# A new order for a PE-bound kernel: PSUM banks from a table, and dummy matmuls one by one

## The chip, the cores and the metric

The kernel runs on one core of one Trainium2 chip. Its time is the device time of one execution in microseconds (us). Three timed runs of the kernel before gave 412.07, 411.61 and 411.92 us, median 411.92. Matmuls run on TensorE (PE), elementwise work on VectorE (DVE), ScalarE (ACT) and GpSimd (POOL); transfers are issued by SyncE (SP) and a few by ACT.

## The reference

Two layers. The first is attention over a sliding window of 64 positions, 8 batches, 8 heads of 64 dimensions, 576 positions. Its output, heads side by side, is x (8 x 576 x 512), the input of a mixture of four experts, each a causal attention with one head; the gate takes the best two of four experts at each position.

```python
scores = scale * q @ k.T;  mask = (rel >= 0) & (rel < 64)
attn = exp(scores - max) / (sum + 1e-9);  x = attn @ v            # layer 1
logits = x @ w_gate;  topk = best 2 of 4;  w = softmax over these # layer 2
for e in range(4):
    a = softmax(causal(scale * (x @ wq[e]) @ (x @ wk[e]).T))
    out += w[e] * (a @ (x @ wv[e]) @ wo[e])       # where e is chosen
```

Everything is float32.

## The kernel before, in words

**Layer 1** (stage 1) works on units of eight tiles. A tile is a pair of heads and a block of 64 query rows; its keys are the block itself and the one before. There are 36 units, u = 0 to 35. `s1_qk(u)` multiplies queries and keys into two PSUM banks. ACT copies the scores of the block before to SBUF (`sm`), DVE adds those of the block itself by a predicated copy (`own` is the mask), DVE takes the row's maximum (`st`), POOL adds it, ACT takes the exponential, DVE sums, ACT and DVE make the reciprocal, POOL multiplies. `s1_t(u)` transposes the result on PE through the identity matrix `ident` (tile `t`); ACT copies it (`ft`), and for the early units DVE and POOL mask it into `pt`. `s1_av(u)` multiplies with the values (tile `o`), and ACT and DVE write the result as a high and a low part in float32r, `xh` and `xl`.

**Layer 2** (stage 2) takes the batches one by one. Each projection is a sum of three float32r products, high by high, high by low, low by high: `v2ps` (values and gate), `kps` and `qps` (keys and queries, two pairs of experts, two halves of the positions). The weights are split once in the same way; `wklo` and `wvlo` are such low parts, written by DVE. Scores (`s` from `kt`, `qt`) go through a custom DVE instruction with the causal mask, ACT's exponential and POOL's multiplication; DVE transposes 32x32 blocks and DMAs move them (`pt` from `st`); a second value product on PE (`o`), and the output projection `ops`. The last batch is transposed on PE.

**What sets the order.** `Plan` records all instructions; matmuls inside one `nc.block` form one entry. `issue()` (line 194 of the profile's file) hands them out in the order of `LIST`, a table with one number for each entry. Every engine executes its own in that order and waits for semaphores; there is no scheduler behind it. In the profile all instructions carry line L203, where `Plan` calls them, so rows are told apart by their tiles.

**PSUM.** Eight banks. All tiles come from one pool with the tag `s` and `bufs=8`; a new tile takes a bank that the pool gives it.

**Dummies.** `warm(k)` issues two matmuls of the identity with itself into a bank that nobody reads; each float32 matmul is two instructions on PE, so one call shows as four. `WARM = 6` calls are in the list, all early.

A name such as `s_3_0` in the order below is `s1_3_0`, the first bank of unit 3's scores (the order drops a digit that follows a letter); the last number counts tiles.

Of the kernel before, what the change touches and what calls it, by code (L numbers as in the profile page):

```python
# [7 lines left out]
F32 = mybir.dt.float32  # L8
# [8 lines left out]
BLK = S // 64  # L17
# [148 lines left out]
)  # L166
TAIL = 2
WARM = 6
BPOS = 0.05
SJOIN = 1  # L170
PARTS = ((0, 5), (5, 9))
# [47 lines left out]
def window_attention_moe_attention(ctx: ExitStack, tc: tile.TileContext, qT, kT, vW,  # L219
# [130 lines left out]
    def tiles(u):  # L350
        for i in range(SIZES[u]):
            yield i % 2, i // 2, *ORDER[STARTS[u] + i]

    def s1_qk(u):

        banks = [psum.tile([128, 4, 128], F32, tag="s", bufs=8, name=f"s1_{u}_{x}") for x in range(2)]
# [612 lines left out]
```

## Time and profile before

| | before |
|---|---|
| median of three timed runs | 411.92 us |
| the profiled execution, whole | 413.24 us |
| its span, first to last instruction | 411.5 us |
| mean granted clock of PE | 0.995 |
| PE busy | 398.9 us, 97% |
| DVE / ACT / POOL busy | 310.7 / 260.5 / 276.7 us |
| dummy matmuls | 24 instructions, 5.2 us |
| DMA | 72.69 MB, 177 GB/s |

The profile shows one execution. PE's matmuls overlap and their ends are modelled, so "busy" says that PE had work and not that it ran at its peak; the time from one start to the next tells the speed. Of the critical chain 87% of the span is PE and 8% DVE. A group "idle before" names what an engine waited for.

### The profile page before, as it was taken

To read this page: it belongs to the slowest core of one execution; us is meant where nothing else is said; L and a number is where in the kernel's file an instruction comes from. 1 tells how busy PE (TensorE), PEld (TensorE's weight loads), DVE (VectorE), ACT (ScalarE), POOL (GpSimd) and SP (SyncE) were. 2 spreads that over 40 slices of the span, in tenths; PEclk is the share of its full clock that TensorE was granted. 3 is DMA by queue.
4 is the path that set the end of the run, shared out by engine and by line. 5 is a ranking of instruction groups with operands and counts; after the bars stand their busy time and mean duration, and the time that the engine had idled before them with its cause. 6 is when DMAs were issued, how large, how long until landed. Compare 5 with 4: busy or idle time off the path is not lost.

```text
span 411.5 us, 14007 instructions
## 1 busy us (share of the span) xinstructions
PE 398.9 (97%) x5308; PEld 358.9 (87%) x5308; DVE 310.7 (75%) x996; ACT 260.5 (63%) x865; POOL 276.7 (67%) x471
## 2 busy tenths in 40 slices
PE   7689999999999999999999999999999999999996
PEld 7479889999988989898989898988988999898875
DVE  3799998889695878879786876969887768445742
ACT  2666657685748485674858567486856676447852
POOL 3868887977797876887786966877768671504420
PEclk9899999999999999999999999999999999999999
DMA  7987346376867475368776669487657613453113
GB/s 240 349 310 268 111 144 231 78 208 181 239 223 203 135 182 217 106 172 267 193 248 143 205 147 308 130 211 197 176 130 222 151 60 80 131 134 103 53 53 127
DMA packets 33363, 72.69 MB, mean 177 GB/s; under 512 B 6160, under 2 KB 10256, under 8 KB 33296
## 3 DMA queue, kind: packets, MB, share of 16 engines
q1 hardware_dynamic: 32640, 71.14, 58.2%
q8 instruction: 42, 0.69, 0.7%
q10 hardware_dynamic: 656, 0.66, 0.5%
q14 instruction: 25, 0.20, 0.2%
HBM read 39.85 MB, written 9.44 MB: 120 GB/s over the span
## 4 chain that ended last, share of the span: by engine, by line
PE 87%; DVE 8%; POOL 2%; ACT 1%; issue 1%; ACTq 0%; POOLq 0%
PE o L203 18%; PE s L203 17%; PE ops L203 12%; PE v2ps L203 12%; PE kps L203 12%; PE qps L203 11%; PE t L203 4%; DVE pt L203 2%; DVE st L203 2%; DVE sm L203 1%; POOL sm L203 1%; PE warm L203 1%; DVE xl L203 1%; ACT sm L203 0%; DVE wklo L203 0%
## 5 line engine op out<-in xcount | busy, mean ns | idle before, releaser
L203 POOL TENSOR_SCALAR p<-p,r,g 128x448 f32<-128x448 f32 (+4 forms) x135 | 84.0, 636 | 29.5 <-DVE r L203 23.8
L203 POOL TENSOR_TENSOR sm<-sm,st 128x512 f32<-128x512 f32 x72 | 76.9, 1070 | 30.1 <-DVE st L203 20.0
L203 POOL TENSOR_SCALAR_AFFINE_SELECT pt<-ft 64x512 f32<-64x512 f32 x126 | 84.2, 668 | 17.5 <-ACT ft L203 8.4
L203 ACT ACTIVATE p<-p,r 128x192 f32<-128x192 f32 (+3 forms) x135 | 78.7, 588 | 16.9 <-DVE r L203 16.7
L203 PE MATMUL o<-pt,v 128*64 128x64 f32 (+2 forms) x1776 | 80.8, 249 | 1.8 <-DVE pt L203 1.2
L203 PEld LDWEIGHTS o<-pt,v 128*64 128x64 f32 x1776 | 68.2, 138 | 15.0 <-issue 3.2
L203 DVE STREAM_TRANSPOSE st<-p 128x128 f32<-128x128 f32 (+5 forms) x126 | 59.9, 515 | 5.7 <-POOL p L203 5.5
L203 DVE CUSTOM_DVE_ANT_0 p<-s,causal 128x320 f32<-128x320 f32 (+2 forms) x120 | 54.3, 483 | 7.8 <-PE s L203 7.3
L203 DVE TENSOR_REDUCE st<-sm 128x8 f32<-128x512 f32 x72 | 48.4, 679 | 7.0 <-ACT sm L203 6.1
L203 PE MATMUL s<-kt,qt 64*128 64x320 f32 (+3 forms) x480 | 43.3, 318 | 0.0
L203 DVE COPY_PREDICATED sm<-own,s 128x256 f32<-128x256 uint8 x72 | 29.3, 442 | 12.9 <-ACT sm L203 7.7
L203 PE MATMUL kps<-xh,wklo 128*128 128x256 f32 (+1 forms) x128 | 37.7, 295 | 1.2 <-DVE wklo L203 1.2
L203 PE MATMUL kps<-xh,wkhi 128*128 128x256 f32 (+1 forms) x128 | 38.7, 302 | 0.0
L203 PE MATMUL qps<-xh,wqhi 128*128 128x320 f32 (+1 forms) x128 | 38.4, 300 | 0.0
L203 PE MATMUL v2ps<-wvhi,xh 128*128 128x260 f32 x128 | 37.7, 294 | 0.2 <-DVE xl L203 0.2
L203 PE MATMUL s<-k,q 64*64 64x128 f32 (+1 forms) x1116 | 37.8, 275 | 0.1
L203 PE MATMUL qps<-xl,wqhi 128*128 128x320 f32 (+1 forms) x128 | 37.6, 294 | 0.0
L203 PE MATMUL kps<-xl,wkhi 128*128 128x256 f32 (+1 forms) x128 | 37.6, 294 | 0.0
L203 PE MATMUL qps<-xh,wqlo 128*128 128x320 f32 (+1 forms) x128 | 37.6, 294 | 0.0
L203 PEld LDWEIGHTS s<-kt,qt 64*128 64x128 f32 x480 | 35.0, 186 | 2.8 <-issue 0.7
L203 PE MATMUL v2ps<-wvhi,xl 128*128 128x260 f32 x128 | 36.2, 283 | 0.0
L203 PE MATMUL v2ps<-wvlo,xh 128*128 128x260 f32 x128 | 36.2, 283 | 0.0
(124 smaller groups left out, 921.6 us busy)
## 6 DMA issues: line engine op xcount, KB each, us to landing
v<-in_vW_dram SPq DMA_DIRECT2D x28, 576.0 KB, 5.2
pt<-st SPq DMA_DIRECT2D x112, 116.0 KB, 2.3
pt<-st SPq DMA_DIRECT2D x112, 80.0 KB, 2.1
out_dram<-out SPq DMA_DIRECT2D x32, 256.0 KB, 2.5
k<-in_kT_dram SPq DMA_DIRECT2D x28, 288.0 KB, 5.0
q<-in_qT_dram SPq DMA_DIRECT2D x28, 288.0 KB, 5.2
v<-in_vW_dram SPq DMA_DIRECT2D x3, 320.0 KB, 5.9
out_dram<-out SPq DMA_DIRECT2D x7, 128.0 KB, 2.5
```

The costliest lines, as they stand in the source:

```text
L203: call(*args, **kw)
```

## The change

- `BANKS`, a string of digits, names the bank of each PSUM tile, in the order in which tiles are made. Each bank has a tag of its own with one buffer (`bank()`), so a tile waits until the tile before it in that bank has been read.
- The scores and the value products of units 0 to 3 are now one list entry for each pair of heads instead of one for all eight tiles (`parts(u)`), so that other work can stand between the pieces.
- `warm(k)` is one matmul instead of two, and `WARM` is 24 instead of 6: 24 dummies in place of 12.
- `LIST` is new from its first number to its last, 2797 entries. So every engine's order differs, in most places by a few positions.

```diff
 LIST = (
-    1, 3, 2, 0, 7, 5, 6, 4, 16, 20, 18, 14, 15, 17, 9, 21, 19, 69, 29, 279, 46, 67, 48, 34, 35, 41, 44, 39, 42, 45,
+    1, 3, 2, 0, 6, 4, 7, 5, 15, 19, 14, 17, 16, 18, 8, 22, 21, 20, 29, 30, 31, 308, 309, 34, 315, 35, 45, 46, 61, 53,
...
+BANKS = (
+    "2150600134050431751546247014523236576301365721057242035652177252136347041470465160577323414673270015"
...
-WARM = 6
+WARM = 24
...
-    psum = ctx.enter_context(tc.tile_pool(name="psum", bufs=2, space=PSUM))
+    psum = ctx.enter_context(tc.tile_pool(name="psum", bufs=1, space=PSUM))
+    numbers = iter(BANKS)
+
+    def bank(shape, name):
+        return psum.tile(shape, F32, tag="s" + next(numbers, "0"), name=name)
...
+    def parts(u):
+        t = list(tiles(u))
+        return [[x for x in t if x[2] == p] for p in sorted({x[2] for x in t})] if u < 4 else [t]
+
     def s1_qk(u):
 
-        banks = [psum.tile([128, 4, 128], F32, tag="s", bufs=8, name=f"s1_{u}_{x}") for x in range(2)]
-        with nc.block("s"):
-            for x, j, p, b in tiles(u):
-                c0 = 64 * int(b == 0)
...
+        banks = [bank([128, 4, 128], f"s1_{u}_{x}") for x in range(2)]
+        for group in parts(u):
+            with nc.block("s"):
+                for x, j, p, b in group:
...
     def s1_av(u):
...
-        with nc.block("a"):
-            for i, (x, j, p, b) in enumerate(tiles(u)):
...
+        for group in parts(u):
+            with nc.block("a"):
+                for x, j, p, b in group:
+                    i = 2 * j + x
...
     def warm(k):
-        ps = psum.tile([128, 512], F32, tag="s", bufs=8, name=f"warm_{k}")
+        ps = bank([128, 512], f"warm_{k}")
         with nc.block("z"):
-            for i in range(2):
-                nc.tensor.matmul(ps[:, 0:128], lhsT=ident, rhs=ident, start=True, stop=True)
+            nc.tensor.matmul(ps[:, 0:128], lhsT=ident, rhs=ident, start=True, stop=True)
```

In all other places `psum.tile(..., tag="s", bufs=8, ...)` becomes `bank(...)`.

**Place 1.** POOL, from the first instruction of the program on; `ident` is the identity that the dummies read, `tri`, `m_f`, `causal` and `below` are constants of the masks. First before:

```order
L203 MEMSET sm_1_115 128x64
L203 ISA
L203 AFFINE_SELECT m_f<-m_f 64x64
L203 MEMSET sm_0_108 128x64
L203 MEMSET sm_1_115 128x64
L203 MEMSET sm_0_108 128x64
L203 MEMSET ident 128x128
L203 AFFINE_SELECT ident<-ident 128x128
L203 MEMSET causal 128x576
```

Now, the same stretch of POOL (`v_1` is a tile for the values of layer 2):

```order
L213 ISA
L213 AFFINE_SELECT tri<-tri 64x64
L213 AFFINE_SELECT m_f<-m_f 64x64
L213 MEMSET causal 128x576
L213 MEMSET ident 128x128
L213 MEMSET v_1_72 64x256
L213 AFFINE_SELECT ident<-ident 128x128
L213 MEMSET sm_1_133 128x64
```

The identity moved behind a select on `tri` and the large fill of `causal`, and a fill of `v_1` stands between its own two instructions; the small fills of `sm` moved behind it.

**Place 2.** PE, around the first transpose `t_0` of stage 1; `s_3` are unit 3's scores, `o_0` is unit 0's value product. First before:

```order
L203 MATMUL warm_101<-ident 128x128 x2
L203 MATMUL t_0_112<-ident,sm_0_108 128x128 x4
L203 MATMUL s_3_0_133<-k_76,q_75 64x128 x2
L203 MATMUL s_3_1_134<-k_76,q_75 64x128 x2
L203 MATMUL s_3_0_133<-k_78,q_77 64x128 x2
...
L203 MATMUL s_3_1_134<-st_69 64x128 x2
L203 MATMUL t_1_122<-ident,sm_1_115 128x128 x4
L203 MATMUL o_0_117<-pt_0_110,v_79 64x64 x8
L203 MATMUL o_0_117<-pt_0_110,v_80 64x64 x8
L203 MATMUL o_1_129<-pt_1_120,v_81 64x64 x8
```

Now:

```order
L213 MATMUL s_3_0_151<-k_76,q_75 64x128 x2
L213 MATMUL s_3_1_152<-k_76,q_75 64x128 x2
L213 MATMUL t_0_130<-ident,sm_0_126 128x128 x4
L213 MATMUL warm_111<-ident 128x128
L213 MATMUL s_3_0_151<-k_78,q_77 64x128 x2
...
L213 MATMUL warm_113<-ident 128x128
L213 MATMUL warm_103<-ident 128x128
L213 MATMUL s_3_1_152<-st_69 64x128 x2
L213 MATMUL t_1_140<-ident,sm_1_133 128x128 x4
L213 MATMUL o_0_135<-pt_0_128,v_80 64x64 x8
L213 MATMUL o_0_135<-pt_0_128,v_79 64x64 x8
L213 MATMUL warm_102<-ident 128x128
```

Unit 3's first piece moved ahead of `t_0`, and three dummies stand between its other pieces; five more follow `o_0`.

**Place 3.** DVE, in the same time; `st_2` and `st_3` are row maxima and sums of units 2 and 3, `wvlo` and `wklo` low parts of weights. First before:

```order
L203 TENSOR_REDUCE st_2_126<-sm_2_125 128x8
L203 TENSOR_TENSOR pt_0_110<-t_0_112,tri 64x4x128
L203 COPY_PREDICATED sm_3_135<-own,s_3_0_133 128x256
L203 COPY_PREDICATED sm_3_135<-own,s_3_1_134 128x256
L203 TENSOR_REDUCE st_3_136<-sm_3_135 128x8
L203 TENSOR_TENSOR pt_0_110<-t_0_112,tri 64x4x128
L203 TENSOR_TENSOR pt_1_120<-t_1_122,tri 64x4x128 x2
```

Now:

```order
L213 TENSOR_REDUCE st_2_144<-sm_2_143 128x8
L213 TENSOR_TENSOR pt_0_128<-t_0_130,tri 64x4x128 x2
L213 COPY_PREDICATED sm_3_153<-own,s_3_0_151 128x256
L213 COPY_PREDICATED sm_3_153<-own,s_3_1_152 128x256
L213 TENSOR_REDUCE st_3_154<-sm_3_153 128x8
L213 TENSOR_TENSOR pt_1_138<-t_1_140,tri 64x4x128 x2
```

The second half of `pt_0` moved ahead of unit 3's predicated copies.

## Rows read from the trace of the kernel before

**Rows 1.** The page's head and its part 1: engine, busy us, share, instructions.

```profile
span 411.5 us, 14007 instructions
...
PE 398.9 (97%) x5308; PEld 358.9 (87%) x5308; DVE 310.7 (75%) x996; ACT 260.5 (63%) x865; POOL 276.7 (67%) x471
```

**Rows 2.** PE's waits: engine and tile, who it waited for, us, times, longest.

```profile
PE t L203 <- POOL sm L203: 3.1, 4, 2.5
PE warm L203 <- POOL ident L203: 2.2, 1, 2.2
PE o L203 <- DVE pt L203: 1.2, 1, 1.2
PE kps L203 <- DVE wklo L203: 1.2, 1, 1.2
PE o L203 <- POOL pt L203: 0.5, 2, 0.3
PE v2ps L203 <- DVE xl L203: 0.2, 1, 0.2
```

**Rows 3.** Busy time of PE by stretch: from:to, length, busy, clock, DMA.

```profile
25.90:40.00 14.10, 14.10 (x210) 1.00 0.70 241
40.00:59.00 19.00, 18.20 (x337) 1.00 0.47 160
59.00:100.00 41.00, 41.00 (x568) 1.00 0.54 165
100.00:403.20 303.20, 303.03 (x3881) 1.00 0.58 165
403.20:411.50 8.30, 4.42 (x25) 0.94 0.45 158
```

**Rows 4.** The same view with all engines, 40 to 60 us (PE, PEld, DVE, ACT, POOL).

```profile
40.00:60.00 20.00, 19.20 (x345) 16.89 (x344) 19.55 (x46) 12.48 (x35) 17.48 (x27) 1.00 0.45 153
```

**Rows 5.** Timeline of POOL, the first 3 us: start, us, what.

```profile
1.58 0.20 POOL L203 MEMSET ident<- 128x128 f32 x1
1.85 0.29 POOL L203 TENSOR_SCALAR_AFFINE_SELECT ident<-ident 128x128 f32<-128x128 f32 x1
2.09 0.58 POOL L203 MEMSET causal<- 128x576 f32 x1
```

**Rows 6.** Timeline of PE, 0 to 40 us.

```profile
2.20 3.78 PE L203 MATMUL warm<-ident 128*128 128x128 f32 x16 [2.20 <-POOL ident L203]
...
10.60 0.71 PE L203 MATMUL warm<-ident 128*128 128x128 f32 x4
13.79 0.66 PE L203 MATMUL t<-ident,sm 128*128 128x128 f32 x4 [2.48 <-POOL sm L203]
14.37 1.56 PE L203 MATMUL s<-k,q 64*64 64x128 f32 x26
...
25.89 0.39 PE L203 MATMUL kps<-xh,wklo 128*128 128x256 f32 x1 [1.19 <-DVE wklo L203]
```

**Rows 7.** Timeline of DVE, 0 to 25 us.

```profile
15.18 0.68 DVE L203 TENSOR_TENSOR pt<-t,tri 64x512 f32<-64x512 f32 x1
16.67 0.78 DVE L203 COPY_PREDICATED sm<-own,s 128x256 f32<-128x256 uint8 x2 [0.81 <-ACT sm L203]
...
24.20 1.64 DVE L203 SCALAR_TENSOR_TENSOR wklo<-pt,wkhi 128x1024 fp32r<-128x1024 f32 x1
```

**Rows 8.** The chain that ended last, in order of time: two v2ps blocks.

```profile
320.67 1.44 PE v2ps L203 x12
...
335.97 1.64 PE v2ps L203 x12
```

**Rows 9.** Granted clock of PE by stretch (columns as in rows 3).

```profile
15.00:16.00 1.00, 1.00 (x24) 0.50 1.02 372
18.00:19.00 1.00, 0.00 (x0) 0.98 1.04 398
```

More of the change, by code (lines that the diff above doesn't have):

```diff
@@ L29 @@
 LIST = (
[136 rows of a table removed]
[138 rows of a table added]
+)
+BANKS = (
+    "2150600134050431751546247014523236576301365721057242035652177252136347041470465160577323414673270015"
+    "3676352411307761524253072345213146176300213573500241065067145426051167216267373053120632465433164750"
+    "7615036212407136012572756306021274765564714230703531451636170217223130651665734214560700332704104243"
+    "5643161065214036720575672241514461735742716524353734716041355432032571065427326754751067231473450541"
+    "6016446357233021775146412073060215655203052617416144170605371260274220444152077066315207641576723041"
+    "7517032456"
 )
 TAIL = 2
-WARM = 6
+WARM = 24
 BPOS = 0.05
@@ L352, in tiles @@
             yield i % 2, i // 2, *ORDER[STARTS[u] + i]
+    def parts(u):
+        t = list(tiles(u))
+        return [[x for x in t if x[2] == p] for p in sorted({x[2] for x in t})] if u < 4 else [t]
     def s1_qk(u):
-        banks = [psum.tile([128, 4, 128], F32, tag="s", bufs=8, name=f"s1_{u}_{x}") for x in range(2)]
-        with nc.block("s"):
-            for x, j, p, b in tiles(u):
-                c0 = 64 * int(b == 0)
-                for h in range(2):
-                    r, o = slice(64 * h, 64 * h + 64), 64 * (h ^ x)
-                    keys = pairs[p][1][r, 64 * b + c0 - 64:64 * b + 64]
-                    nc.tensor.matmul(banks[x][o:o + 64, j, c0:], lhsT=pairs[p][0][r, 64 * b:64 * b + 64],
-                                     rhs=keys, start=True, stop=True)
+        banks = [bank([128, 4, 128], f"s1_{u}_{x}") for x in range(2)]
+        for group in parts(u):
+            with nc.block("s"):
+                for x, j, p, b in group:
+                    c0 = 64 * int(b == 0)
+                    for h in range(2):
+                        r, o = slice(64 * h, 64 * h + 64), 64 * (h ^ x)
+                        keys = pairs[p][1][r, 64 * b + c0 - 64:64 * b + 64]
+                        nc.tensor.matmul(banks[x][o:o + 64, j, c0:], lhsT=pairs[p][0][r, 64 * b:64 * b + 64],
+                                         rhs=keys, start=True, stop=True)
         n, w = SIZES[u], SIZES[u] // 2
@@ L399, in s1_t @@
         if early:
-            ps = psum.tile([128, 4, 128], F32, tag="s", bufs=8, name=f"t1_{u}")[:, :m]
+            ps = bank([128, 4, 128], f"t1_{u}")[:, :m]
             with nc.block("t"):
@@ L405, in s1_t @@
         else:
-            banks = [psum.tile([128, 8, 64], F32, tag="s", bufs=8, name=f"t1_{u}_{o}")[:, :m] for o in range(2)]
+            banks = [bank([128, 8, 64], f"t1_{u}_{o}")[:, :m] for o in range(2)]
             with nc.block("y"):
@@ L431, in s1_av @@
         size, w, start = SIZES[u], SIZES[u] // 2, STARTS[u]
-        o = psum.tile([128, 8, 64], F32, tag="s", bufs=8, name=f"o1_{u}")
-        with nc.block("a"):
-            for i, (x, j, p, b) in enumerate(tiles(u)):
-                for h in range(2):
-                    c = 64 * (h ^ x)
-                    k = x * w + j
-                    nc.tensor.matmul(o[64 * h:64 * h + 64, i], lhsT=pairs[p][2][h, b],
-                                     rhs=t[:, k // 2, k % 2, c:c + 64], start=True, stop=True)
-                if b == BLK - 1 and later(p):
-                    freed.append(p)
+        o = bank([128, 8, 64], f"o1_{u}")
+        for group in parts(u):
+            with nc.block("a"):
+                for x, j, p, b in group:
+                    i = 2 * j + x
+                    for h in range(2):
+                        c = 64 * (h ^ x)
+                        k = x * w + j
+                        nc.tensor.matmul(o[64 * h:64 * h + 64, i], lhsT=pairs[p][2][h, b],
+                                         rhs=t[:, k // 2, k % 2, c:c + 64], start=True, stop=True)
+                    if b == BLK - 1 and later(p):
+                        freed.append(p)
         i = 0
@@ L540, in warm @@
     def warm(k):
-        ps = psum.tile([128, 512], F32, tag="s", bufs=8, name=f"warm_{k}")
+        ps = bank([128, 512], f"warm_{k}")
         with nc.block("z"):
-            for i in range(2):
-                nc.tensor.matmul(ps[:, 0:128], lhsT=ident, rhs=ident, start=True, stop=True)
+            nc.tensor.matmul(ps[:, 0:128], lhsT=ident, rhs=ident, start=True, stop=True)
     def s2_v(b, j):
-        ps = psum.tile([128, 512], F32, tag="s", bufs=8, name=f"v2ps_{b}_{j}")
+        ps = bank([128, 512], f"v2ps_{b}_{j}")
         with nc.block("VW"[j // 4]):
@@ L604, in proj @@
         c0, n = HALVES[b > 0][half]
-        ps = psum.tile([128, 512], F32, tag="s", bufs=8, name=f"{name}ps_{b}_{pr}_{half}")
+        ps = bank([128, 512], f"{name}ps_{b}_{pr}_{half}")
         w = slice(128 * pr, 128 * pr + 128)
@@ L643, in s2_mm @@
     def s2_mm(b, pr, k):
-        banks = SB[b, pr, k] = [psum.tile([128, 512], F32, tag="s", bufs=8, name=f"s2_{b}_{pr}_{k}_{e}")
+        banks = SB[b, pr, k] = [bank([128, 512], f"s2_{b}_{pr}_{k}_{e}")
                                 for e in range(2)]
@@ L725, in s2_tp @@
             s0, w, m = group[0][0], group[0][1].shape[1], len(group)
-            ps = psum.tile([128, 512], F32, tag="s", bufs=8, name=f"t2_{b}_{pr}_{part}_{k}")
+            ps = bank([128, 512], f"t2_{b}_{pr}_{part}_{k}")
             with nc.block("TU"[part]):
@@ L780, in s2_av_mm @@
         n = 64 * (b1 - b0)
-        o = OB[b, pr, part] = psum.tile([128, 512], F32, tag="s", bufs=8, name=f"o2_{b}_{pr}_{part}")
+        o = OB[b, pr, part] = bank([128, 512], f"o2_{b}_{pr}_{part}")
         with nc.block("AB"[part]):
@@ L809, in s2_o @@
         end = b == NB - 1 and j == 4
-        banks = [psum.tile([128, DM // (1 + end)], F32, tag="s", bufs=8, name=f"ops_{b}_{j}_{i}") for i in range(1 + end)]
+        banks = [bank([128, DM], f"ops_{b}_{j}_{i}")[:, 0:DM // (1 + end)] for i in range(1 + end)]
         for letter, prs in (("O", (0, 1)),) if b < NB - 1 else (("o", (0,)), ("O", (1,))):
```

272 rows, old and new, of the table LIST are left out of this document.

## The prediction

> **What bounds the kernel now.** I read the page's head first, then PE's waits, then PE by stretches, and only then the single instructions of the first 26 us. The head says that PE is busy for 398.9 of 411.5 us and DVE for 310.7 [rows 1], so no more than 12.6 us of PE's span is idle at all. The waits say where some of it lies [rows 2]: 2.2 us for the identity matrix that the dummy matmuls read, 3.1 us in front of transposes (2.5 us in one piece), 1.2 and 0.5 us for pt, 1.2 us for wklo. The stretches say the rest [rows 3]: between 59 and 403.2 us PE has 0.17 us idle in 344; between 40 and 59 us it has 0.8 us; the last 8.3 us hold 3.9 us in which PE has finished and the last copies and output transfers run. So the kernel is PE's list of work, with idle time only ahead of 59 us and at the very end. From 20 to 60 us a second engine sets the pace: DVE is busy for 19.55 of the 20 us from 40 to 60 [rows 4], and PE fills in around it. A change of order can therefore win only ahead of 59 us; behind that it can win nothing but the price of switching between kinds of matmul, and it can lose wherever it makes a wait.
>
> **The change, part by part.** The arithmetic is untouched: the same matmuls on PE, the same instructions on DVE, the same bytes. Only dummies are added, 24 single ones for 6 pairs.
>
> *The first dummy.* It waits for the identity on POOL: filled at 1.58, cut out at 1.85, done at 2.14 [rows 5], PE starts at 2.20. In the new order two selects of 64 rows and the fill of 128x576 stand ahead of that fill, and another fill between it and its select. POOL's first select there waits for DVE's second fill, by my estimate at 1.3. From there by the rows: two selects at 0.24 (start to start), 0.51 for the large fill (from its start to the next one; its row is 0.58), two fills at 0.27, 0.29 for the last select: the identity is ready at 3.1, and PE starts some 0.85 us later.
>
> *The dummies ahead of the first scores.* 16 matmul instructions took 3.78 us, 0.24 each [rows 6]. Seven single dummies are 14 instructions, so 0.45 us less. The first scores, whose loads are in by then in both, come 0.4 us later. In unit 0, DVE's first predicated copy now follows ScalarE's second copy and not its first; I take 0.15 us (between 0 and 0.4, since ScalarE's three copies for DVE's first start are all that stand there). t_0, the first real transpose, stands at the end of one chain DVE, POOL, ACT, DVE, POOL with no slack, and moves from 13.79 to about 14.35.
>
> *From t_0 to wklo.* DVE has its largest hole here: 0.81 us ahead of the copies of unit 3 at 16.67, which wait for ScalarE and so for the scores s_3, all of which PE starts only at 14.37, behind t_0 [rows 6, 7]. In the new order both halves of pt_0 stand ahead of those copies, and one half is 0.68 us, which fills most of the hole. But s_3 is now cut by dummies: one behind t_0, two more ahead of its last piece. At the half clock these six instructions take 0.24 us each, 1.4 us, on the very path by which unit 3 reaches DVE; I make the hole 0.55 us. So DVE gains 0.25 of the 0.55 us that t_0 lost, and wklo ends not at 25.84 [rows 7] but at 26.15. PE's first projection, which stands waiting for it in both orders, goes on at 26.2 and not at 25.89: +0.3 us. Bounds: at the full clock (four in 0.71 us [rows 6]) the six dummies take 1.1 and the scores behind them less too, the hole is gone, and wklo ends at 25.6 (-0.25); if two holes of 0.81 stand there it is +1.1.
>
> *The other dummies.* All 24 stand ahead of the first projection, and so does the same real work as before: units 0 to 5's scores, t_0 to t_2, o_0, o_1. Until 25.89 PE waits for DVE in any case, so the twelve further dummies cost nothing but what is counted above; what hides them is the idle ahead of t_0 (2.48 us), ahead of o (1.2) and ahead of kps (1.2). Without that cover they would cost 24 instructions at 0.18 to 0.24 us, 4.3 to 5.8 us.
>
> *From 25.9 to 59 us.* DVE's list holds the same instructions, in nearly the same order; so does PE's, with kps_1_0 alone at the front and two units of scores later. The 0.8 us idle [rows 3] can go or double: -0.8 to +1.0. I take 0, as DVE at 98% [rows 4] leaves no order that is much better.
>
> *From 59 us to the end.* PE is full, so its time is the sum of its blocks. A change between float32 and float32r matmuls costs: twelve v2ps matmuls take 1.44 us behind kps and 1.64 behind o [rows 8], so 0.2 us for going in and out, 0.1 for each boundary. Behind the last wait for DVE the old order has 104 such boundaries, the new one 102: -0.2 us. The last 24 output matmuls stand in the same order; only the transposes ahead of them are dealt out differently. I take 0 there, from -0.2 to +0.5.
>
> *Banks.* So far the pool gave each PSUM tile a free bank; now a table does. No wait of PE in the old trace is for a bank. Counting PE work from the last write of a bank to the first of its next tile, the old order has 20 places behind 30 us with under 1.2 us, the new one 32. In the old trace such places made no idle, so I take 0; at worst the twelve cost 0.1 us each, +1.2.
>
> *Sum.* +0.3 (start) + 0 - 0.2 (boundaries) + 0 + 0 = +0.1 us on the span of 411.5, so 411.6. The profiled execution took 413.24 as a whole, 1.7 more than its span and 1.3 more than the median of the three timed runs; the difference goes onto that median: 411.92 + 0.1 = 412.0.
>
> [...]
>
> **Rivals.** (a) *Faster.* The dummies keep the clock up through s_3, and the new order also closes the waits behind 26 us: -0.25 at the start, -0.8 for the idle, -0.2 for boundaries, 410.7. For it: the idle is there to be taken [rows 2, 3]. Against: the largest piece, ahead of t_0, is a chain through DVE, POOL and ACT that no dummy shortens, and the 0.85 us of the identity is lost first. (b) *Slower.* A block in the full stretch behind 59 us finds its bank not yet read. Each such wait moves the end by its own length, since PE has no idle left to take it up [rows 3]. The place: the first value product of batch 1 takes the bank of a v2ps that PE leaves 0.54 us of work earlier, and eleven more are tighter than 1.2 us. It decides as soon as ACT or DVE has a queue of one instruction more than in the old order; at 0.1 us each, +1.2, on top of 412.0: 413.2. Against: places as tight in the old order cost nothing. (c) *The dummies don't do what they are for*, the clock falls all the same: that is the forecast itself, 412.0.
>
> **How the numbers follow.** This kernel's runs tell a difference of about 0.2%, 0.8 us, from none. The forecast, from 411.2 to 412.7, has 0.45: the start's bounds are -0.25 and +1.1, and most of that stays within it. Case (a) and other gains have 0.30, case (b) and new waits between 26 and 59 us have 0.25. The range goes from (a), with a little more of the idle taken, to (b): 410.3 to 413.4.
>
> **What would show it.** Right: PE's first dummy at about 3.0; t_0 near 14.3, still behind more than 2 us of idle; half clock during s_3; the first projection's wait for wklo ending near 26; PE full from 59 us; the tail as before. Wrong: wklo's end ahead of 25 or behind 27; PE waits behind 59 us, whose releaser is an ACT or DVE read of another tile; or an end stretch longer than 8.3 us.

## The result, and the profile after

The changed kernel takes 415.36 us (median of 19 runs, 411.76 to 417.81) against 412.07 us of the kernel before beside it (19 runs, 410.63 to 413.94). The ratio is 1.0080, with a 95% interval from 1.0054 to 1.0106: slower by 0.8%, outside the forecast range of 410.3 to 413.4 us. The ratio of e2_ident_first, further down, leaves out three of its twelve runs as slow (416.1 to 417.6 us); over all twelve its median would give 1.0029.

The profiled execution has a span of 415.7 us, 4.2 more than before. As a whole it took 417.47 us and is one of the changed kernel's slowest. The head, against [rows 1]:

```profile
span 415.7 us, 14089 instructions
PE 403.0 (97%) x5332; PEld 363.2 (87%) x5332; DVE 306.1 (74%) x996; ACT 260.4 (63%) x865; POOL 275.3 (66%) x471
```

PE's waits, against [rows 2] (engine and tile, whom it waited for, us, times, longest):

```profile
...
PE t L213 <- POOL below L213: 1.8, 1, 1.8
PE t L213 <- ACT out L213: 1.1, 1, 1.1
...
PE s L213 <- DVE yl L213: 0.3, 1, 0.3
PE t L213 <- ACT qf L213: 0.3, 1, 0.3
...
PE s L213 <- DVE xl L213: 0.2, 1, 0.2
```

The waits for wklo and for DVE's pt are gone from the list. New are waits of transposes for ScalarE (out, qf) and of scores for VectorE (yl, xl). PE by stretch, against [rows 3], says where they are:

```profile
25.90:40.00 14.10, 13.98 (x222) 1.00 0.73 241
40.00:59.00 19.00, 18.33 (x340) 1.00 0.58 188
59.00:100.00 41.00, 40.62 (x562) 1.00 0.53 158
100.00:200.00 100.00, 99.67 (x1465) 1.00 0.67 192
200.00:300.00 100.00, 97.85 (x1283) 0.98 0.67 191
300.00:403.20 103.20, 103.20 (x1112) 1.00 0.42 114
```

Between 200 and 300 us PE is idle for 2.15 us, and its mean clock is 0.98. In the kernel before, PE had 0.17 us idle in all of 100 to 403 us, at 1.00. The timeline of PE at that place (start, us, what, idle before and its releaser):

```profile
228.65 4.83 PE L213 MATMUL o<-pt,v 128*64 128x256 f32 x108
234.56 0.25 PE L213 MATMUL t<-ident,sm 64*128 64x64 f32 x1 [1.08 <-ACT out L213]
235.08 0.46 PE L213 MATMUL t<-ident,sm 64*128 64x64 f32 x7 [0.27 <-ACT qf L213]
235.69 0.35 PE L213 MATMUL s<-kt,qt 64*128 64x192 f32 x1 [0.15 <-DVE xl L213]
236.34 1.04 PE L213 MATMUL s<-kt,qt 64*128 64x192 f32 x11 [0.31 <-DVE yl L213]
237.32 1.38 PE L213 MATMUL s<-k,q 64*64 64x128 f32 x30
```

PE is idle for 1.8 us in these four waits. From start to start they cost 2.7 us, since the matmuls between them start one by one: from the `o` block to the `s` block of keys and queries `k,q` it is 8.67 us here and 5.99 us in the trace of the first experiment (e1_out_early), where the same matmuls wait for nothing:

```profile
228.42 4.83 PE L220 MATMUL o<-pt,v 128*64 128x256 f32 x108
...
234.41 0.99 PE L220 MATMUL s<-k,q 64*64 64x128 f32 x30
```

Four releasers in a row, and they have one cause. ScalarE in the changed kernel:

```profile
230.25 0.59 ACT L213 ACTIVATE out<-ops 128x512 f32<-128x512 f32 x1
233.82 0.60 ACT L213 ACTIVATE out<-ops 128x512 f32<-128x512 f32 x1 [2.98 <-DMA out_dram<-out]
234.32 0.59 ACT L213 ACTIVATE xh<-o 128x512 fp32r<-128x512 f32 x1
234.79 0.23 ACT L213 ACTIVATE qf<-qps 128x64 f32<-128x64 f32 x1
```

The second copy of an output block waits 2.98 us for an `out` tile. There are two buffers (tag "out"), and the transfer that empties the one it needs has not landed. xh, qf, qt, yh and ft stand behind that copy and start only after it. In the trace xh starts at 234.32 us, right behind the copy at 233.82, qf at 234.79 and ft at 235.58. DVE's xl and yl stand behind these (DVE is idle for 4.13 us ahead of xl at 234.94), and PE behind all of them. SP's queue shows why the transfer is late; before first, after second:

```profile
212.90 0.51 SPq L203 DMA_DIRECT2D pt<-st  x1
213.51 0.53 SPq L203 DMA_DIRECT2D out_dram<-out  x1
214.09 10.37 SPq L203 DMA_DIRECT2D pt<-st  x15
224.50 0.59 SPq L203 DMA_DIRECT2D k<-in_kT_dram  x1
225.19 0.40 SPq L203 DMA_DIRECT2D out_dram<-out  x1
```

```profile
213.28 11.40 SPq L213 DMA_DIRECT2D pt<-st  x16
224.72 0.58 SPq L213 DMA_DIRECT2D v<-in_vW_dram  x1
225.40 0.39 SPq L213 DMA_DIRECT2D out_dram<-out  x1
225.83 0.96 SPq L213 DMA_DIRECT2D k<-in_kT_dram  x2
226.90 0.50 SPq L213 DMA_DIRECT2D out_dram<-out  x1
```

The two output transfers are those of batch 2, rows 128 to 255 and then 0 to 127. Before, the first went out among the pt transfers and the second behind one k load. Now both stand behind all sixteen pt transfers and a v load, and the second also behind two k loads. It is issued at 226.90 us and lands at 233.8.

Behind the stall the granted clock falls (PE alone: stretch, busy, clock, DMA share, GB/s):

```profile
234.00:237.70 3.70, 2.41 (x34) 1.00 0.17 41
237.80:241.20 3.40, 3.40 (x39) 0.50 0.58 138
```

PE is full in the second stretch at a granted clock of 0.50, so those 3.4 us count as 1.7 us at 1.00; matmul by matmul against e1_out_early, which has no such stretch there, 1.5 us are lost in it. At the start of the kernel the same view, against [rows 9], and PE's timeline, against [rows 6]:

```profile
16.00:19.30 3.30, 3.30 (x29) 0.50 1.04 389
```

```profile
3.35 3.35 PE L213 MATMUL warm<-ident 128*128 128x128 f32 x14 [3.35 <-POOL ident L213]
6.63 1.99 PE L213 MATMUL s<-k,q 64*64 64x64 f32 x32
...
15.05 0.66 PE L213 MATMUL t<-ident,sm 128*128 128x128 f32 x4 [1.81 <-POOL below L213]
...
27.11 0.38 PE L213 MATMUL kps<-xh,wklo 128*128 128x256 f32 x1
```

The projection that stood until 25.89 us runs at 27.11. PE's timeline counts no wait there, because the matmul ahead of it, begun at 26.87, is still shown busy. But the projection starts 0.05 us after DVE has written wklo, as in the kernel before, and so DVE's chain sets it in both. The first row of each fence is unit 1's sum. Behind it DVE waits once: before by 0.81 us at 16.67 us [rows 7], after by 0.92 us ahead of its copy of unit 3's scores. Before first, after second:

```profile
12.93 0.69 DVE L203 TENSOR_REDUCE st<-sm 128x8 f32<-128x512 f32 x1 [0.32 <-ACT sm L203]
```

```profile
14.61 0.69 DVE L213 TENSOR_REDUCE st<-sm 128x8 f32<-128x512 f32 x1 [0.74 <-ACT sm L213]
...
19.61 0.44 DVE L213 COPY_PREDICATED sm<-own,s 128x256 f32<-128x256 uint8 x1 [0.92 <-ACT sm L213]
...
25.84 1.22 DVE L213 SCALAR_TENSOR_TENSOR wklo<-pt,wkhi 128x1024 fp32r<-128x1024 f32 x1
```

Where the start ends can be fixed by the block of value products at which PE waits for DVE for the last time; in both kernels the same 814 matmuls (dummies not counted) stand ahead of it. Before first, after second:

```profile
58.86 0.39 PE L203 MATMUL v2ps<-wvhi,xh 128*128 128x260 f32 x1 [0.21 <-DVE xl L203]
```

```profile
59.95 0.39 PE L213 MATMUL v2ps<-wvhi,xh 128*128 128x260 f32 x1 [0.20 <-DVE r L213]
```

The start costs 1.1 us in this trace. From there to PE's last matmul it is 348.8 us before and 351.9 after, 3.1 us more. The parts can be read against e9_third_out_buffer (below), where the changed order has no wait over 0.15 us in that stretch and takes 346.7 us. Matmul by matmul, the changed kernel loses 5.2 us to it: 2.7 us in the waits at 234 to 237 us, 1.5 us to the clock behind them, and about 1 us in smaller waits at 152.9, 169.9 and 288.0 us. The kernel before loses 2.1 us to it, but 0.9 us of that belongs to its one profiled execution: in three other traces of the old order (e8, e10, e14) the stretch is 347.8 to 347.9 us. So where nothing waits the new order is shorter by about 1 us.

### The profile page after: what moved, and what is told of

It reads as the page before. It is cut to its first block, busy times and chain, and to the rows that moved or that the text cites. A ratio compares the mean times of both kernels' runs of the same rounds, so it can differ in the third digit from the quotient of the medians.

```text
span 415.7 us, 14089 instructions
## 1 busy us (share of the span) xinstructions
PE 403.0 (97%) x5332; PEld 363.2 (87%) x5332; DVE 306.1 (74%) x996; ACT 260.4 (63%) x865; POOL 275.3 (66%) x471
## 4 chain that ended last, share of the span: by engine, by line
PE 84%; DVE 5%; POOL 4%; ACT 2%; DMA 2%; issue 2%; SPq 0%; POOLq 0%; DVEq 0%
PE s L213 17%; PE o L213 16%; PE v2ps L213 12%; PE kps L213 11%; PE qps L213 11%; PE ops L213 10%; PE t L213 4%; PE warm L213 2%; DVE st L213 2%; DMA out_dram<-out 2%; POOL p L213 1%; POOL sm L213 1%; DVE sm L213 1%; ACT p L213 1%; DVE pt L213 1%
## 5 line engine op out<-in xcount | busy, mean ns | idle before, releaser
L213 ACT ACTIVATE p<-p,r 128x448 f32<-128x448 f32 (+4 forms) x135 | 78.2, 583 | 13.5 <-DVE r L213 12.9
L213 PE MATMUL o<-pt,v 128*64 128x64 f32 (+2 forms) x1776 | 79.9, 248 | 0.9 <-POOL pt L213 0.6
L213 PEld LDWEIGHTS o<-pt,v 128*64 128x64 f32 x1776 | 68.3, 138 | 13.1 <-issue 1.3
L213 DVE STREAM_TRANSPOSE st<-p 128x128 f32<-128x128 f32 (+5 forms) x126 | 61.0, 518 | 3.0 <-POOL p L213 2.6
L213 DVE TENSOR_REDUCE st<-sm 128x8 f32<-128x512 f32 x72 | 48.3, 676 | 12.9 <-ACT sm L213 12.2
L213 PE MATMUL kps<-xh,wkhi 128*128 128x320 f32 (+1 forms) x128 | 38.6, 301 | 0.0
L213 PE MATMUL kps<-xh,wklo 128*128 128x320 f32 (+1 forms) x128 | 37.8, 295 | 0.0
L213 PE MATMUL kps<-xl,wkhi 128*128 128x320 f32 (+1 forms) x128 | 37.6, 294 | 0.0
## 6 DMA issues: line engine op xcount, KB each, us to landing
q<-in_qT_dram SPq DMA_DIRECT2D x28, 288.0 KB, 4.3
k<-in_kT_dram SPq DMA_DIRECT2D x28, 288.0 KB, 5.1
```

The source lines that it names most:

```text
L213: call(*args, **kw)
```

## The experiments

The theory was that two places cost the time: A1, the `out` tile of batch 2, with the clock behind it, and A2, the start. Rivals were the bank table, the start alone, and dummies that keep or fail to keep the clock. Entries of LIST were moved or left out by two tables, read in `Plan.issue`:

```diff
-        for n in LIST:
+        order = list(LIST)
+        for n, m in MOVES:
+            order.remove(n)
+            order.insert(order.index(m), n)
+        for n in order:
+            if n in DROP:
+                continue
             for call, args, kw in self.ops[n]:
                 call(*args, **kw)
```

Ratios are to the kernel before, run beside each group on the same chip (its medians there: 412.96, 412.33, 413.16 and 412.84 us), so ratios compare better than microseconds from group to group.

| run | edit | us | ratio (95%) |
|---|---|---|---|
| changed kernel | | 415.36 | 1.0080 (1.0054 to 1.0106) |
| e1_out_early | output transfers earlier | 413.35 | 0.9996 (0.9973 to 1.0020) |
| e2_ident_first | identity first | 414.14 | 1.0010 (0.9978 to 1.0043) |
| e3_pool_banks | banks from the pool | 415.72 | 1.0068 (1.0039 to 1.0096) |
| e4_few_dummies | identity first, 4 dummy instructions at the front | 412.11 | 0.9977 (0.9957 to 0.9997) |
| e5_all_three | e1 and e4 | 411.00 | 0.9977 (0.9960 to 0.9994) |
| e6_no_dummies | e1, identity first, no dummies | 409.26 | 0.9938 (0.9919 to 0.9957) |
| e7_before_late_out | kernel before, output transfer later | 415.50 | 1.0082 (1.0049 to 1.0114) |
| e8_before_few_dummies | kernel before, 4 dummy instructions at the front | 411.61 | 0.9992 (0.9975 to 1.0008) |
| e9_third_out_buffer | three `out` buffers | 411.40 | 0.9959 (0.9941 to 0.9978) |
| e10_before_no_dummies | kernel before, no dummies | 412.44 | 0.9982 (0.9965 to 1.0000) |
| e11_no_dummies_alone | no dummies | 410.64 | 0.9949 (0.9931 to 0.9968) |
| e12_best_pool_banks | e6, banks from the pool | 411.09 | 0.9957 (0.9938 to 0.9975) |
| e13_no_dummies_third_buffer | no dummies, three `out` buffers | 409.39 | 0.9912 (0.9899 to 0.9925) |
| e14_before_third_buffer | kernel before, three `out` buffers | 412.34 | 0.9987 (0.9974 to 1.0000) |

**Output transfers earlier.** Entries 1493 and 1472 are the two transfers, 1563 is the v load.

```diff
+MOVES = ((1493, 1563), (1472, 1563),)  # (entry, entry that it is put in front of)
```

> The changed kernel with two output transfers of batch 2 (rows 128 to 255 and 0 to 127) put one place earlier on SP's queue: behind the sixteen pt<-st transfers, but ahead of the v load and the two k loads that they follow now. Nothing else moves. Theory A (ScalarE stands in line behind a free `out` buffer: its copy out<-ops at 233.8 us waited 2.98 us for an output transfer, and xh, qf and yh behind it held VectorE, GpSimd and then TensorE, 2.2 us of PE waits between 234.5 and 236.8 us and a half-clock stretch at 237.8 us): the idle time before that copy falls from 2.98 us to under 0.5 us, the PE waits at 234 to 237 us fall from 2.2 us to under 0.5 us, no half-clock stretch follows them, and the median falls by 2 to 4 us, from 415.4 to 411.5 to 413.5 us. Rival B (the bank table holds TensorE there): the PE waits stay at 2 us and the time at 415.4 us within 0.8 us. Rival C (the loss is at the start alone): the waits go, but the time falls by less than 1 us.

SP's queue and ScalarE in its trace:

```profile
213.04 11.10 SPq L220 DMA_DIRECT2D pt<-st  x16
224.25 1.02 SPq L220 DMA_DIRECT2D out_dram<-out  x2
```

```profile
230.02 1.08 ACT L220 ACTIVATE out<-ops 128x512 f32<-128x512 f32 x2
230.97 0.62 ACT L220 ACTIVATE xh<-o 128x512 fp32r<-128x512 f32 x1
```

The transfers leave 1.2 and 2.0 us earlier, the two copies follow each other without a gap, and PE's four waits are gone, as theory A had it. The time falls by 0.84% by the ratios (2.0 us between medians of two groups). No run has a mean clock under 0.994, while eight of the changed kernel's nineteen have 0.990 or 0.991, and these eight are its slowest (416.5 to 417.8 us).

**A third buffer, in the changed kernel and in the one before.**

```diff
-        tag, bufs = ("out", 2) if b < NB - 1 or j % 2 else ("sm1", 3)
+        tag, bufs = ("out", 3) if b < NB - 1 or j % 2 else ("sm1", 3)
```

> The changed kernel with three buffers instead of two for the `out` tiles; the order of the work is untouched, so the output transfers of batch 2 land as late as before. Theory A (ScalarE waits for a free `out` buffer): the copy out<-ops at 230 us follows the one before it at once, PE's 2.2 us of waits at 234 to 237 us are gone, and the median falls by as much as with the transfers put earlier, to 412.8 to 414.0 us (2.0 us less there). Rival F (what counted there was the load on the DMA queues, not the buffer): 415.4 us within 0.6 us.

> The kernel before with three buffers instead of two for the `out` tiles. Theory A (in the order of before no copy waits for an `out` buffer where TensorE needs ScalarE): ratio to the kernel before 0.998 to 1.002. Rival J (a third buffer helps any order, so that its gain does not single out the changed order): ratio 0.996 or less, as for the changed kernel, which it brought from 1.008 to 0.996.

In the changed kernel the transfer lands as late as ever, 6.6 us after its issue at 224.2 us, and nothing waits for it:

```profile
227.49 1.08 ACT L213 ACTIVATE out<-ops 128x512 f32<-128x512 f32 x2
228.44 0.62 ACT L213 ACTIVATE xh<-o 128x512 fp32r<-128x512 f32 x1
```

1.2% less by the ratios (4.0 us between medians), more than was expected. About 0.6 us beyond e1_out_early is from smaller waits: the trace of e1_out_early still has 0.2 us at 169.6 and 0.4 us at 283.6 us, this one none over 0.15 us, and at a mean clock of 1.000 its runs take 410.1 to 410.7 us against 410.9 to 411.3. Part of the rest goes with the clock: six of its twelve runs have a mean clock of 1.000, against three of twelve. That the edit brings this about is not shown. The kernel before gains 0.1% from the same edit, at the edge of its interval, where the changed kernel gains 1.2%. So the wait belongs to the new order.

**The late transfer put into the kernel before.** Entry 1444 is the output of rows 0 to 127 of batch 2; it goes behind the next two v loads.

```diff
+MOVES = ((1444, 1691),)  # (entry, entry that it is put in front of)
```

> The kernel before with one transfer moved: the output of rows 0 to 127 of batch 2 stands on SP's queue behind the next two v loads instead of ahead of them (issued at about 230.2 us instead of 225.2, landing at about 234 to 235 us instead of 228.5). Theory A: ScalarE's copy out<-ops, at 232.6 us before, waits for it until 234 to 235 us; yh and xh behind it are late by as much, PE waits 1 to 2.5 us between 233 and 238 us, and in part of the runs a half-clock stretch follows (1.7 us); median 1.5 to 4 us above the kernel before. Rival B (only the bank table makes such a wait reach TensorE) or rival E (slack of ScalarE's work hides it): within 0.5 us of the kernel before.

```profile
233.10 0.60 ACT L210 ACTIVATE out<-ops 128x512 f32<-128x512 f32 x1 [2.45 <-DMA out_dram<-out]
```

```profile
233.75 1.09 PE L210 MATMUL s<-k,q 64*64 64x128 f32 x28 [0.72 <-ACT out L210]
...
235.51 0.39 PE L210 MATMUL v2ps<-wvhi,xh 128*128 128x260 f32 x1 [0.58 <-DVE xl L210]
```

One transfer moved by two places makes the kernel before as slow as the changed one: +3.2 us, ratio 1.0082. The profiled run was its fastest (412.47 us, 1.3 us of waits of PE and no fall of the clock behind them); the other five took 414.4 to 417.3 us. The bank table has no part in it, since this kernel has none.

**Banks from the pool.**

```diff
-        return psum.tile(shape, F32, tag="s" + next(numbers, "0"), name=name)
+        return psum.tile(shape, F32, tag="s", bufs=8, name=name)
```

> The changed kernel with the table of PSUM banks taken out: each PSUM tile takes a bank from one pool of eight again, as in the kernel before; the order of the work is that of the changed kernel. Theory A (banks cost nothing, ScalarE waits for the `out` buffer): the wait of 2.9 us before out<-ops at 233 to 234 us stays, PE waits 1 to 2.5 us behind it, and the time is 415.4 us within 0.8 us. Rival B (banks from the table hold blocks): the time falls by 1.2 us or more, to under 414.2 us, and the PE waits at 234 us for ACT out<-ops and qf go while ScalarE's own wait stays.

> The kernel of the run without dummies (identity first, output transfers of batch 2 earlier, no dummy entries) with the table of banks taken out: banks from one pool of eight, as in the kernel before. This order has runs within 0.6 us of each other, so that 0.2% shows. Theory A (the table costs nothing): 409.3 us within 0.5 us. Rival B (blocks wait for their banks because of the table): 408.8 us or less. Rival I (the table gains something that the late transfer hid): 409.9 us or more, with more waits of TensorE for ACT or DVE behind 59 us.

In e3_pool_banks ScalarE's wait stays at 2.48 us, and PE still waits for it. The time does not fall; the table is not the cause. On the order without dummies, whose runs lie within 0.6 us, the pool's banks cost 0.2% against the table (0.9957 against 0.9938; the intervals overlap), and PE has waits of 0.4 us at 291 us for ScalarE's ft, 0.2 us at 127 and 0.4 us at 375 us that the table doesn't have. If anything the table gains something, as rival I had it.

**The start: identity and dummies.** Entries 34 and 35 fill and cut the identity, 31 is the first select on POOL; 39 to 62 are the 24 dummies; in the kernel before 39 to 44 are its six pairs.

```diff
+MOVES = ((34, 31), (35, 31),)  # e2_ident_first, e4_few_dummies; with the two of e1 in e5_all_three, e6_no_dummies
+DROP = (46, 61, 53, 59, 56)  # e4_few_dummies, e5_all_three
+DROP = (39, 40, 41, 42, 43, 44, 45, 46, 47, 48, 49, 50, 51, 52, 53, 54, 55, 56, 57, 58, 59, 60, 61, 62)  # e6, e11, e12, e13
+DROP = (44, 39, 42)  # e8_before_few_dummies
+DROP = (39, 40, 41, 42, 43, 44)  # e10_before_no_dummies
```

> The changed kernel with the memset and the select of the identity put at the front of GpSimd's order, ahead of the two selects and the memset of `causal` that they follow now. Theory A (1.1 us of the loss is the start: identity at 3.3 instead of 2.2 us, and the dummies in front of the first scores push these back): the first dummy starts at about 1.4 us instead of 3.35, the first scores at about 4.7 instead of 6.63 (k lands at 4.3 us), t_0 1.2 to 1.9 us earlier than 15.05, and the median falls by 1.1 to 1.9 us, to 413.5 to 414.3 us; the stall at 234 us stays. Rival C' (the first projections wait for the weights anyway, so that the start is hidden): time 415.4 us within 0.5 us, with PE waiting about 1 us for wklo or wkhi before 27 us.

> The changed kernel with five of the seven dummy entries in front of the first scores left out, so that 4 dummy instructions stand there instead of 14, and with the identity at the front of GpSimd's order as in the second run. Theory A: the first scores start when k has landed, at about 4.35 us, 0.3 to 0.4 us earlier than with all seven; the time is that of the second run or up to 0.4 us less, and the clock at 15 to 20 us is granted as in the changed kernel. Rival D (these dummies keep the clock up): TensorE runs at half clock before 15 us, or one half-clock stretch more appears, and the time is 1.5 us or more above that of the second run.

> The changed kernel with the three edits together: the two output transfers of batch 2 ahead of the loads, the identity first on GpSimd, five of the seven dummy entries in front of the first scores left out. Theory A (two places of the order cost the time: the start, and ScalarE's copy that waits for an output transfer): the times add as far as they did not overlap; no wait of out<-ops at 230 us in any run, first scores at about 4.35 us, median 410.3 to 411.8 us against 415.4 of the changed kernel and 412.1 of the run with few dummies. Rival (the run with few dummies has lost the wait already, because its transfers lie otherwise): 412.1 us within 0.3 us.

> The changed kernel with the output transfers of batch 2 earlier and the identity first, and with all 24 dummy entries left out. Theory A (the dummies in front of the first scores delay them, those behind them lie in idle time): TensorE starts its scores when k lands, at about 4.3 us; the half rate lasts longer (in the run with few dummies the granted clock was full from 7.4 us on, with fourteen dummies from 1.4 us on it was full from 5.5 us on), which costs the first scores up to 1.5 us, and a second half-clock stretch between 10 and 25 us costs up to 1.7 us: 411.5 to 414.0 us. Rival D' (dummies do nothing for the clock): the time of the run with all three edits or up to 0.5 us less, 410.0 to 411.5 us. In neither case does the clock fall between 30 and 400 us.

> The kernel before with three of the four dummy entries (two matmuls each) in front of the first scores left out: 4 dummy instructions instead of 16. Theory A (in both kernels the dummies, not the loads, set the first scores): the first scores start at about 4.1 us (q lands at 4.02 us) instead of 5.91, t_0 1.0 to 1.7 us earlier than 13.79. Then either the first projections follow (time 0.8 to 1.5 us less than before, wait for wklo unchanged), or, as the forecast read the rows, VectorE's chain to wklo ends at 25.8 us all the same (time within 0.4 us, PE's wait for wklo 2 us or more instead of 1.19).

> The kernel before with all six dummy entries (twelve matmuls) left out. Theory A (dummies delay the blocks behind them more than their clock gives back, in either order of the work): the first scores start at about 4.1 us, t_0 about 12.6 us, median 410.0 to 411.3 us against 411.6 of the kernel before with three of them left out and 412.7 of the kernel before as it is. Rival D (the dummies of the kernel before pay for themselves): 411.6 to 413 us. Rival G (what the order annealed anew gains is real, and hidden in the changed kernel by the dummies and the late transfer): this kernel stays 1 us or more above the 409.26 us of the changed kernel without dummies and with its transfers earlier.

> The changed kernel with all 24 dummy entries left out and nothing else: the identity stays behind `causal` on GpSimd, the output transfers of batch 2 stay behind the loads. Theory A (two costs, start and transfer, that add): 409.3 us of the run without dummies, plus between 0 and 3.9 us for the wait of out<-ops, as it comes out in each run: median 410.0 to 412.0 us, runs spread over 2 us or more where they were within 0.6 us with the transfers earlier. Rival H (the dummies are the whole loss): within 0.4 us of 409.26 us. Rival (the identity matters without dummies): t_0 later than 12.8 us.

> The changed kernel with all 24 dummy entries left out and three buffers for the `out` tiles; order, identity and transfers otherwise as in the changed kernel. Theory A (dummies and the wait for an `out` buffer are the loss): as the run without dummies and with the earlier transfers (ratio to the kernel before 0.9938) or up to 0.7 us less, since the third buffer took 0.7 us more than the earlier transfers at the same clock: ratio 0.992 to 0.994, runs within 1 us of each other, no wait of out<-ops for an output transfer. Rival (identity and order of the transfers had a part of their own in that run): 0.995 or more.

From the trace of one run of each (us; half clock is the stretch at a granted clock of 0.50 between 12 and 24 us, for e10 by the duration of its instructions; e3 differs from the changed kernel only in the banks, e7 from the kernel before only in a transfer at 228 us; the last but one column is DVE's wait between unit 1's sum and wklo):

| kernel | dummy instructions | first scores | t_0 | half clock | unit 1's sum | wait of DVE | first projection with wklo |
|---|---|---|---|---|---|---|---|
| before | 24 | 5.91 | 13.79 | 14.6 to 18.0 | 12.93 | 0.81 | 25.89 |
| e7, before | 24 | 5.56 | 12.66 | 18.8 to 22.2 | 11.79 | none | 24.07 |
| e8, before | 12 | 4.33 | 12.62 | none | 12.21 | 0.81 | 24.88 |
| e10, before | 0 | 4.10 | 13.06 | to 22.6 | 12.66 | 1.01 | 25.82 |
| after | 48 | 6.63 | 15.05 | 15.9 to 19.3 | 14.61 | 0.92 | 27.11 |
| e3 | 48 | 6.64 | 14.20 | none | 13.49 | none | 24.97 |
| e9 | 48 | 6.63 | 14.33 | none | 13.63 | none | 25.12 |
| e2, identity first | 48 | 4.70 | 12.63 | none | 11.92 | none | 23.40 |
| e4, identity first | 38 | 4.35 | 13.04 | 14.3 to 17.7 | 12.62 | 0.56 | 25.01 |
| e5, identity first | 38 | 4.44 | 13.54 | none | 13.13 | none | 24.61 |
| e6, identity first | 0 | 4.36 | 12.78 | 13.1 to 16.5 | 12.14 | none | 23.61 |
| e11 | 0 | 4.39 | 12.81 | 14.1 to 20.9 | 11.95 | none | 23.67 |
| e13 | 0 | 4.37 | 12.79 | none | 11.92 | none | 23.40 |

In all sixteen traces the projection starts 0.05 to 0.06 us after DVE has written wklo, with dummies or without. So DVE's chain sets it, and the dummies count by what they do to that chain: they hold back the scores that it waits for. In the new order DVE takes 11.4 us from unit 1's sum to the end of wklo wherever no score of unit 3 comes late (11.7 in e11); the kernel before takes 12.9 with its wait. The changed kernel's trace has a wait again (12.5 us), and unit 1's sum is 1.7 us later than before: ahead of it stand the later identity, unit 0's scores at the lower rate (6.63 to 8.54 us, in e9 to 7.82), and six dummy instructions (8.54 to 9.66 us) between the scores of units 0 and 1.

Without dummies the new order has its weights 2.2 to 2.5 us earlier than the kernel before in its trace, whatever the clock does: e6_no_dummies and e13_no_dummies_third_buffer (first fence and second):

```profile
4.36 1.99 PE L225 MATMUL s<-k,q 64*64 64x64 f32 x32 [4.36 <-DMA k<-in_kT_dram]
...
23.61 0.38 PE L225 MATMUL kps<-xh,wklo 128*128 128x256 f32 x1 [0.54 <-DVE wklo L225]
```

```profile
23.40 0.39 PE L218 MATMUL kps<-xh,wklo 128*128 128x256 f32 x1 [0.52 <-DVE wklo L218]
```

With dummies a late identity costs 1.7 us (e9 against e2, both without a fall of the clock), and a half-clock stretch up to 2.0 us (27.11 against 25.12 with 48 dummy instructions, 25.01 against 24.61 with 38). Without dummies 6.8 us at half clock cost 0.3 us (e11 against e13): unit 3's scores still reach DVE in time. Dummies at the front do bring the full rate sooner, by the duration of the instructions (the six behind the first scores take 0.86 us in e2 and 1.58 in e5, with ten fewer in front; the projection runs at 23.40 and 24.61), but with none at all it is as early. The old order varies too: where unit 3's scores ran at full clock its projection came at 24.07 (e7). Compared at like clock, the changed kernel's start is late by 0.9 to 1.2 us (e3 and e9 against e7, after against before).

The times say the same. Leaving out all dummies instead of five of them is worth 1.7 us in one group (411.00 to 409.26). Left out alone (e11_no_dummies_alone) they take the ratio from 1.0080 to 0.9949, about as much as the third buffer alone (0.9959); both together reach 0.9912, so the two gains overlap. In e11's trace ScalarE's wait is 1.08 us and PE's behind it 0.3 us. Its runs still spread over 2.3 us; without dummies and without that wait they lie within 0.6 us (e6) and 0.4 us (e13, at clocks from 0.992 to 1.000), those of the changed kernel within 6 us. In the kernel before, leaving all dummies out moves the time by 0.2% (0.9982, 0.9965 to 1.0000).

Several expectations missed. e6_no_dummies came out under both of its cases: the dummies are no cover that the clock needs, they are a cost (409.26 us without them, 411.00 with 38 of their instructions). e10_before_no_dummies missed its theory A: in the old order they cost next to nothing, as rival D had it, and as rival G had it that kernel stays 3 us above e6. e4_few_dummies fell 2.0 us under e2_ident_first, not 0.4 at most: its trace has ScalarE's wait at 0.82 us instead of 2.98 and PE's at 0.2 us. e5_all_three has the same ratio, so the earlier transfers added nothing to it, as the rival in that expectation had it. e8_before_few_dummies came earlier by 1.0 us at the projection and by less in the time. e2_ident_first had t_0 2.4 us earlier, more than expected, and gained 3.7 us at the projection but 0.5 to 0.7% in the time: the wait at 231 us stayed, in its trace with a half-clock stretch behind it. e13_no_dummies_third_buffer came out just under its range of ratios.

e13_no_dummies_third_buffer has the lowest ratio: 409.39 us, 0.9912 (0.9899 to 0.9925), with none of e6's moves. That is the changed order and its table of banks, without the dummies and with one buffer more; it beats both kernels.

## Why the prediction was wrong, step by step

- *The first dummy.* Identity at 3.1 us: it was 3.30, and PE started 1.15 us later instead of 0.85. Right in kind, short by 0.3 us.
- *The dummies ahead of the first scores.* +0.4 us foreseen, +0.72 measured (6.63 against 5.91). t_0 foreseen at 14.35, measured at 15.05. In e9, with the same instructions here, it is at 14.33; there the first 32 score matmuls take 1.19 us (6.63 to 7.82) instead of 1.91, so the rest is the lower rate of PE in this one trace.
- *From t_0 to wklo.* wklo foreseen to end at 26.15 us; it ended at 27.05. The path was right: DVE's chain sets the projection, and unit 3's scores, cut by dummies, hold it. The sizes were not: four dummy instructions at the granted clock of 0.50 take 1.15 us from start to start (17.30 to 18.45), 0.29 each instead of 0.24, the hole is 0.92 us instead of 0.55, and unit 1's sum comes 1.7 us later, where t_0 was to move by 0.55. At the full clock the hole is gone, as the lower bound had it, and wklo ends at 24.92 (e3) and 25.06 (e9), ahead of its 25.6.
- *The other dummies.* **This step failed.** It said that twelve further dummies cost nothing, since PE waits for DVE until 25.89 us in any case. But DVE itself waits for scores that stand on PE's queue behind dummies, so that its end moves with them; the six instructions between units 0's and 1's scores (1.12 us) were put at nothing. In the old order leaving all dummies out changes nothing at 25.8 us (e10), in the new one the projection goes from 27.11 to 23.4 to 23.7. The sum gave the start +0.3 us, with an upper bound of +1.1; it measured +1.1 to +1.2, and without dummies it would have been -2.2 to -2.5.
- *From 25.9 to 59 us.* 0 foreseen; the difference is 1.2 us at 27 us and 1.1 at 60 us. Right.
- *From 59 us to the end.* **The step that failed most.** "PE is full, so its time is the sum of its blocks" looked at PE's blocks alone. Their sum fell by about 1 us rather than 0.2 (346.7 us in e9 against 347.8 to 347.9 in e8, e10 and e14; one trace each), but the order of SP's queue was never read: two output transfers had moved behind loads, and the copy that waits for them stands on ScalarE ahead of xh and yh. That cost 2.7 us of waits and, in part of the runs, 1.5 us of clock. Taking it away gained 0.84% (e1) or 1.2% (e9), and putting it into the kernel before cost 0.82% (e7).
- *The tail.* From PE's last matmul to the end 3.9 us before and after. Right.
- *Banks.* 0, at worst +1.2: right, and the sign may be a gain (e12).
- *The clock.* Half clock during s_3 was foreseen and came: a granted clock of 0.50 from 15.9 to 19.3 us, before from 14.6 to 18.0. It does not come in each run: the changed kernel's nineteen have mean clocks of 0.990 to 1.000, and the traces of e2, e3 and e9 have no fall at the start. What sets its moment was not shown. The second fall, in the middle of the full stretch, was not foreseen at all; it stands in three traces (after, e2, e3), each time behind the stall, and in no trace without a stall.

Of the rivals, (b) had the right form: something in the full stretch waits for a buffer, and the wait moves the end by its own length. But it named PSUM banks, priced at 0.1 us each, where it was one SBUF buffer and a transfer, 2.7 us and the clock. A gain such as (a) was in the new order as well, -2.2 to -2.5 us at the start and about -1 behind 59 us, but without the dummies that (a) counted on; they and the one wait turned it round. Two of the signs of being wrong came up: wklo's end behind 27 us, and waits behind 59 us for ScalarE and VectorE. Not settled is how much of the remaining spread of the changed kernel, at one clock, is the transfer's landing alone: at 1.000 its three runs differ by 1.9 us, those of e1 by 0.4 us.

## What to carry to other kernels

When a change reorders everything, compare the DMA queue too: for each transfer that frees a buffer, find the next writer of that buffer and what stands behind it on that writer's engine. An instruction on an engine that waits is free only as long as nothing behind it is what the other engine waits for; price it again along the new chain (without dummies the projection came at 23.4 to 23.7 us instead of 27.11 here, in the old order at 25.82 instead of 25.89). A stall in a stretch where the matmul engine was full cost 2.7 us in its waits here and, in the trace of the changed kernel, 1.5 us in the clock behind it, so one more buffer where copies wait on transfers (1.2% here) is worth trying first.

## What the runs showed of the hardware

- A stretch of 3.4 us at a granted clock of 0.50 cost 1.5 us where PE was full (after against e1, from 237.8 us). One of 6.8 us cost 0.3 us at the first projection where PE waited for others anyway (e11 against e13). The runs of e13 at mean clocks of 0.992 and 1.000 differ by under 0.4 us, those of e9 at 0.996 and 1.000 by 2.0 us.
- The granted clock fell from 1.00 to 0.50 at 237.8 us after waits of PE of 1.1, 0.3, 0.2 and 0.3 us between 233 and 237 us, and behind the same stall in e2 (234.2 us) and e3 (235.3 us); in e7 waits of 0.7 and 0.6 us were not followed by a fall.
- PE's first matmul that reads wklo started 0.05 to 0.06 us after VectorE's write of it ended, in all sixteen traces.
- An output transfer of 256 KB issued behind three loads took 6.9 us to land (226.9 to 233.8 us), ahead of them 2.3 and 2.6 us (e1).
- In the kernel before without dummies PE ran at the lower rate until 22.6 us by the duration of its instructions (t_0's four transposes 1.11 us instead of 0.66; four such transposes took 1.12 us at a granted clock of 0.50 in the kernel before with its dummies, at 16.11 us), while the trace's granted clock reads 1.00 from 12 to 24 us, and the projection still ran at 25.82 us.
